# Retention and channel mix on one core: attention in 64x64 array tiles, two tokens per partition, one written order

## The chip, the cores and the metric

The kernel runs on one core of one Trainium2 chip. The metric is the device time of a launch in microseconds (us); lower is better. Engines are named as the profile does: PE is TensorE (PEld its weight loads), DVE is VectorE, ACT is ScalarE, POOL is GpSimd, SP is SyncE.

## The reference

Four sequences of 768 tokens, eight heads of 64 values. The first half is a decaying linear attention, the second a gated channel mix on its output.

```python
# attention: B, H, S, D = 4, 8, 768, 64
gamma = 1.0 - 2.0 ** (-5.0 - np.arange(H))
for t in range(S):
    state = gamma * state + outer(k[:, :, t], v[:, :, t])      # per batch and head, 64 x 64
    y[:, :, t] = (1 / sqrt(D)) * (q[:, :, t] @ state)
# channel mix: x is y with the heads side by side, 512 wide; x_prev is x one token back (0 at first)
xk = mu_k * x + (1 - mu_k) * x_prev
xr = mu_r * x + (1 - mu_r) * x_prev
k2 = relu(xk @ w_k) ** 2                                       # 512 -> 1024
out = sigmoid(xr @ w_r) * (k2 @ w_v)                           # 1024 -> 512
```

All inputs and the output are 32-bit floats in device memory.

## The kernel before

Attention works on chunks of 128 tokens, 24 of them, six to a sequence; loads and the channel mix work on blocks of 256 tokens, 12 of them. Tokens lie on the partitions: a chunk's q, k and v are tiles of 128 tokens by 8 heads by 64. q and v are loaded by GpSimd's queue and cast to 16 bits on the way, one DMA for each chunk; k comes in 32 bits through SP's queue (the first four chunks through GpSimd's).

For each chunk: `scale_k` (L179) multiplies k by powers of gamma. `transposes` (L190) turns q and the scaled k, two heads at a time, with an identity matrix on the full 128x128 array, and `transposed` (L194) copies the result from PSUM on ScalarE. `scores` (L201) multiplies k by q for each head, 64 rows of the array at a time, so that two heads use the two halves of its rows. `masked` (L209) applies the causal mask on VectorE. `state` (L222, L230) adds the chunk's k-v sums to the state in PSUM; before an even chunk the kept state is put back by a matmul with the identity. `kept` (L238) takes the state out on VectorE. `result` adds the state's part of y (L249, full array) and the chunk's own part (L255, half of the array's columns for each head). `decayed` (L266) applies the remaining decay and writes y, turned, to `xT`.

The mix has these steps for each block: `differ` (L280) takes x minus x_prev, on GpSimd except for the first two blocks; `mixed` (L288) makes xk and xr on VectorE, four instructions of 128x256 each; `keys` (L299) is xk times w_k in 32 matmuls of 256 columns; `squared` (L309, L310) is relu and square on ScalarE; `gate` (L316) is xr times w_r in 8 matmuls of 512 columns; `opened` (L323) is the sigmoid; `values` (L331) is k2 times w_v in 16 matmuls of 512 columns; `store` (L340, L345) multiplies the two on VectorE and sends the rows out by SP's queue.

PSUM's eight banks are split into two pools of four: `psa` for attention, `psm` for the mix. Each step is put in a plan with a time, from the tables `ORDER["att"]`, `ORDER["mix"]` and `ORDER["start"]` on a grid of 12 units per block; the plan is sorted by time, and every engine's instructions are written in that order. Nothing is reordered after that (`manual_schedule`).

Of the kernel before, what the change touches and what calls it, by code (L numbers as in the profile page):

```python
# [9 lines left out]
F16 = mybir.dt.float16  # L10
# [5 lines left out]
ORDER = {  # L16
    "att": {
        "scale": (-11.82,),
        "first": (-6.14, 0.23),
        "T": (-2.09, 2.5),  # L20
        "TC": (-0.47, 4.83),
        "S": (2.27, 4.47),
        "SE": (3.82, 11.21),
        "A": (3.18, 6.35),
        "M": (5.96, 7.66),
        "Y": (8.04, 9.34),
        "YE": (8.05, 9.72),
        "dx": (11.71,),
        "xk": (18.04, 21.12),
        "xr": (21.16, 27.83),  # L30
    },
    "mix": {
        "G": (-1.27, -0.4, 3.31, 4.49),
        "K": (0.71, 3.37, 5.32, 9.07),
        "R": (5.49, 5.1),
        "RS": (9.95, 9.96),
        "V": (7.7, 9.1, 4.91, 9.14),
        "O": (12.13, 13.29),
    },
    "load": (1.19, 3.99),  # L40
    "pw": (-105.55, -78.0),
    "start": {
        0: (-6.29, -4.12, -3.14, -2.71),
        1: (-5.55, -2.96, -2.96, 0.0),
        2: (-3.52, 0.96, 0.84, 1.45),
        3: (-0.17, 2.67, 1.83, 3.0),
    },
}
# [3 lines left out]
def kernel(  # L52
# [18 lines left out]
    NCH = S // C  # L71
# [3 lines left out]
    TM = 2 * C  # L75
    NBLK = B * S // TM
    COLS = S + 1
    LOG = 7
    NC = B * NCH


    gam = 1.0 - 2.0 ** (-5.0 - np.arange(H, dtype=np.float64))
    ar = np.arange(C, dtype=np.float64)
    causal_np = (ar[None, :] >= ar[:, None]).astype(np.float16)
    c16_np = np.concatenate([np.eye(P, dtype=np.float16), causal_np], axis=1)

    gk_np = np.concatenate([gam[None, :] ** (C - ar[:, None]), gam[None, :] ** (-ar[:, None])], axis=1)
    h_pj = 2 * np.arange(NJ)[None, :] + (np.arange(P) // D)[:, None]
    pw_np = gam[h_pj][:, None, :] ** (2.0 ** np.arange(LOG)[None, :, None])
    half = (np.arange(2)[None, :] == (np.arange(P) // D)[:, None]).astype(np.float64)  # L90
    one = np.ones((P, NJ))
    gs_np = np.stack([w[:, :, None] * half[:, None, :] for w in (one, gam[h_pj] ** TM)], axis=1)
    g0_np = np.stack([0.125 * KSC * gam[h_pj] ** -C, gam[h_pj] ** C], axis=1)
    small_np = np.concatenate(
        [x.reshape(P, -1) for x in (gk_np, gs_np, g0_np, pw_np)], axis=1
# [4 lines left out]
    def pool(name, bufs, **kw):  # L100
        return ctx.enter_context(tc.tile_pool(name=name, bufs=bufs, **kw))

    const = pool("const", 1)
    ld = pool("ld", 5)
    ldk = pool("ldk", 2)
    att = pool("att", 4)
    mid = pool("mid", 2)
    mix = pool("mix", 3)
    outp = pool("outp", 5)
    PS = bass.MemoryType.PSUM  # L110
    psa = pool("psa", 4, space=PS)
    psm = pool("psm", 4, space=PS)

    c16 = const.tile([P, 2 * P], F16, name="c16_sb")
    csm = const.tile([P, 2 * H + (6 + LOG) * NJ], F32, name="csm_sb")
    gy = const.tile([P, 2, NJ, C], F32, name="gy_sb")
# [7 lines left out]
    causal = c16[:, P : 2 * P]  # L124
    gk = csm[:, 0 : 2 * H].rearrange("p (e h) -> p e h", e=2)
    o = 2 * H
    gs = csm[:, o : o + 4 * NJ].rearrange("p (e j h) -> p e j h", e=2, j=NJ)
    o += 4 * NJ
    g0 = csm[:, o : o + 2 * NJ].rearrange("p (e j) -> p e j", e=2)
    o += 2 * NJ  # L130
    pw = csm[:, o:].rearrange("p (l j) -> p l j", l=LOG)
# [3 lines left out]
    K32, Q16, V16, KS, PT, QKT, PA, A2 = {}, {}, {}, {}, {}, {}, {}, {}  # L135
    PSS, SBD, PY, DX, XK, XR, K2, RS, PV = {}, {}, {}, {}, {}, {}, {}, {}, {}
    PZ, PR = {}, {}


    plan = []  # L140
    done = set()

    def needs(*marks):
        assert done.issuperset(marks), marks

    def at(t, fn, *args):
        plan.append((t, len(plan), fn, args))

    def tok(c):
        b, ci = divmod(c, NCH)  # L150
        return b, slice(ci * C, ci * C + C)


    def rows(x, n):
        b, t0 = 2 * n // NCH, 2 * n % NCH * C
        return x[b, :, t0 : t0 + TM, :].rearrange("h (c t) d -> t c h d", t=C)

    def load(n, c, x, eng, tiles, name, dt):

        if n not in tiles:  # L160
            tiles[n] = (ldk if dt is F32 else ld).tile([P, 2, H, D], dt, name=name)
        for i in range(2) if c is None else (c,):
            eng.dma_start(out=tiles[n][:, i], in_=rows(x, n)[:, i])  # L163

    def load_k(n, c=None):
        load(n, c, k, nc.sync if c is None else nc.gpsimd, K32, "k32", F32)

    def load_q(n, c=None):
        load(n, c, q, nc.gpsimd, Q16, "q16", F16)

    def load_v(n, c=None):
        load(n, c, v, nc.gpsimd, V16, "v16", F16)

    def scale_k(n, c, eng):
        if n not in KS:
            KS[n] = att.tile([P, 2, H, D], F16, name="ks16")
        e = slice(0, 2) if c is None else slice(c, c + 1)
        w = gk[:, e, :, None].to_broadcast([P, e.stop - e.start, H, D])
        eng.tensor_tensor(out=KS[n][:, e], in0=K32[n][:, e], in1=w, op=ALU.mult)  # L179
        done.update(("ks", 2 * n + i) for i in range(e.start, e.stop))  # L180

    def heads(tiles, c, a, n):
        return tiles[c // 2][:, c % 2, a : a + n, :]

    def transposes(c):
        PT[c] = psa.tile([P, 2, NJ, C], F16, name="pT", tag="a")
        needs(("ks", c))
        for i, src in enumerate((Q16, KS)):
            for j in range(NJ):
                nc.tensor.transpose(PT[c][:, i, j, :], heads(src, c, 2 * j, 2), ident)  # L190

    def transposed(c):
        QKT[c] = att.tile([P, 2, NJ, C], F16, name="qkT")
        nc.scalar.copy(out=QKT[c], in_=PT.pop(c))  # L194

    def scores(c):
        PA[c] = [psa.tile([P, NJ, C], F32, name=f"pA{hp}", tag="a") for hp in range(2)]
        for j in range(NJ):
            for hp in range(2):
                r = slice(hp * D, hp * D + D)  # L200
                nc.tensor.matmul(  # L201
                    PA[c][hp][:, j, :], lhsT=QKT[c][r, 1, j, :], rhs=QKT[c][r, 0, j, :],
                    start=(j == 0), stop=(j == NJ - 1), skip_group_check=True,
                )

    def masked(c):
        A2[c] = att.tile([P, 2, NJ, C], F16, name="a2t")
        for hp in range(2):
            nc.vector.tensor_tensor(  # L209
                out=A2[c][:, hp], in0=PA[c][hp], in1=causal[:, None, :].to_broadcast([P, NJ, C]),  # L210
                op=ALU.mult,
            )
        PA.pop(c)

    def state(c):
        needs(("ks", c))
        first = c % NCH == 0
        even = c % 2 == 0
        if even:
            PSS[c] = psa.tile([P, NJ, 2 * D], F32, name="pS", tag="a")  # L220
            if not first:
                nc.tensor.matmul(  # L222
                    PSS[c], lhsT=ident, rhs=SBD[c - 1], start=True, stop=False,
                    skip_group_check=True,
                )
        else:
            needs(("kept", c - 1))
            PSS[c] = PSS[c - 1]
        for j in range(NJ):
            nc.tensor.matmul(  # L230
                PSS[c][:, j, :], lhsT=heads(KS, c, 2 * j, 2), rhs=heads(V16, c, 2 * j, 2),
                start=(first and j == 0), stop=(j == NJ - 1), skip_group_check=True,
            )

    def kept(c):
        done.add(("kept", c))
        SBD[c] = att.tile([P, NJ, 2 * D], F16, name="sbd")
        nc.vector.tensor_tensor(  # L238
            out=SBD[c].rearrange("p j (h d) -> p j h d", h=2),
            in0=PSS[c].rearrange("p j (h d) -> p j h d", h=2),  # L240
            in1=gs[:, c % 2, :, :, None].to_broadcast([P, NJ, 2, D]), op=ALU.mult,
        )

    def result(c):
        first = c % NCH == 0
        PY[c] = psa.tile([P, NJ, C], F32, name="pY", tag="a")
        if not first:
            for j in range(NJ):
                nc.tensor.matmul(  # L249
                    PY[c][:, j, :], lhsT=SBD[c - 1][:, j, :], rhs=QKT[c][:, 0, j, :],  # L250
                    start=(j == 0), stop=False, skip_group_check=True,
                )
        for j in range(NJ):
            for hp in range(2):
                nc.tensor.matmul(  # L255
                    PY[c][hp * D : hp * D + D, j, :], lhsT=heads(V16, c, 2 * j + hp, 1),
# [25 lines left out]
    def mixed(m, dst, mu, name, half):  # L282
        xprev = shifted(m)[1]
        if m not in dst:
            dst[m] = mix.tile([P, NJ, TM], F16, name=name)
# [212 lines left out]
```

## Time and profile before

| | before |
|---|---|
| median of 3 runs | 175.91 us (175.77 to 176.37) |
| the profiled execution: span from first to last instruction | 173.1 us |
| between this span and the runs' median | 2.8 us |
| PE busy, matmuls | 155.5 us (90%), 1416 |
| DVE busy | 132.6 us (77%) |
| ACT busy | 92.3 us (53%) |
| POOL busy, its DMA issues among it | 87.7 us (51%) |
| mean granted clock of TensorE | 0.975 |

The page lists each engine's busy time and then the span in 40 slices of about 4.3 us, one digit for each: tenths of the slice in which the engine was busy, or, for PEclk, tenths of the full clock. The chain of waits goes back from the last instruction to what released each step; a row is the start, the duration and the group of instructions. In a timeline row the duration runs from the first start to the last end of the group, so rows of pipelined instructions overlap. In the groups, the last columns are busy time, mean duration of one instruction, and the idle time before them with what ended it.

### The profile page before, as it was taken

Reading aid. Unit: us, or ns where it says so; the run is one execution under the profiler, and the core shown is the slowest. Engines: PE = TensorE matmul, PEld = TensorE weight load, DVE = VectorE, ACT = ScalarE, POOL = GpSimd, SP = SyncE. Lnnn points to the kernel's source line nnn. Section 1 sums busy time; section 2 is a strip of 40 time slices with the busy share of each in tenths; the row PEclk is TensorE's granted clock in tenths of the full one; section 3 lists DMA queues with packets and bytes.
Section 4 is the critical chain, followed back from the end, with each engine's and each line's share of the span. In section 5 each row is a group of like instructions: output and inputs, shape, how many; then the busy total and the mean of one; then the engine's idle time right before and its main releaser. Section 6 shows DMA issues by size and latency. Waiting matters only on the chain.

```text
span 173.1 us, 3480 instructions
## 1 busy us (share of the span) xinstructions
PE 155.5 (90%) x1416; PEld 100.7 (58%) x1416; DVE 132.6 (77%) x232; ACT 92.3 (53%) x146; POOL 87.7 (51%) x81
## 2 busy tenths in 40 slices
PE   0367699879899999999999999999999999999990
PEld 0245457655547557758558468477476486584840
DVE  4459999858698967698799799798799696894312
ACT  3121208929223936827719719639459268275750
POOL 7999340059909990796909709629443040040000
PEclk9999957999999999999999999999999999999998
DMA  6999999997999999379892992993913011030303
GB/s 49 189 178 215 205 167 164 193 199 75 121 215 187 168 209 205 92 101 189 112 201 71 132 170 66 152 153 125 110 21 115 0 56 69 0 121 4 121 0 123
DMA packets 78496, 21.83 MB, mean 126 GB/s; under 512 B 72464, under 2 KB 75152, under 8 KB 78480
## 3 DMA queue, kind: packets, MB, share of 16 engines
q0 software_dynamic: 52880, 9.97, 67.9%
q1 hardware_dynamic: 24544, 11.64, 27.4%
q8 instruction: 11, 0.18, 0.4%
q10 hardware_dynamic: 1056, 0.00, 0.3%
q14 instruction: 5, 0.04, 0.1%
HBM read 24.22 MB, written 6.29 MB: 176 GB/s over the span
## 4 chain that ended last, share of the span: by engine, by line
PE 70%; POOL 10%; issue 8%; DMA 8%; ACT 1%; DVE 0%; POOLq 0%; DVEq 0%
PE pV L331 23%; PE pZ L299 21%; PE pR L316 10%; DMA wk<-in_moe_w_k_dram 5%; PE pT L190 5%; PE pY L255 4%; PE pA L201 3%; POOL q L163 3%; DMA v<-in_v_dram 3%; POOL ks L179 2%; PE pY L249 2%; POOL k L163 2%; POOL v L163 2%; PE pS L230 2%; POOL dx L280 1%
## 5 line engine op out<-in xcount | busy, mean ns | idle before, releaser
L280 POOL TENSOR_TENSOR dx<-xT 128x1024 f32<-128x1024 f32 x10 | 18.9, 1890 | 62.8 <-DVE xT L266 62.8
L299 PE MATMUL pZ<-xk,wk 128*128 128x256 f16 x384 | 48.6, 280 | 0.2 <-DVE xk L288 0.2
L331 PE MATMUL pV<-wv,k 128*128 128x512 f16 x192 | 46.7, 380 | 0.0
L194 ACT COPY qkT<-pT 128x1024 f16<-128x1024 f16 x24 | 24.1, 1006 | 40.8 <-PE pT L190 40.7
L299 PEld LDWEIGHTS <-wk 128*128 128x128 f16 x384 | 37.2, 100 | 7.7 <-issue 0.9
L309 ACT ACTIVATE kr<-pZ 128x512 f32<-128x512 f32 x48 | 28.4, 591 | 22.3 <-PE pZ L299 22.3
L209 DVE TENSOR_TENSOR a2t<-pA,c_sb 128x512 f16<-128x512 f32 x48 | 30.6, 681 | 10.8 <-PE pA L201 10.7
L310 ACT ACTIVATE k<-kr 128x512 f16<-128x512 f32 x48 | 30.2, 630 | 1.5
L288 DVE SCALAR_TENSOR_TENSOR xr<-dx,mur,xT 128x256 f16<-128x256 f32 x48 | 29.0, 646 | 0.0
L331 PEld LDWEIGHTS <-k 128*128 128x128 f16 x192 | 17.3, 98 | 17.9
L288 DVE SCALAR_TENSOR_TENSOR xk<-dx,muk,xT 128x256 f16<-128x256 f32 x48 | 25.4, 574 | 2.0 <-POOL dx L280 2.0
L340 DVE SCALAR_TENSOR_TENSOR osb<-pV,rsb 128x512 f32<-128x512 f32 x24 | 15.8, 684 | 11.8 <-ACT rsb L323 8.5
L316 PE MATMUL pR<-wr,xr 128*128 128x512 f16 x96 | 23.0, 379 | 0.7 <-DMA wr<-in_moe_w_r_dram 0.7
L163 POOL DMA_DIRECT2D q<-in_q_dram x24 | 22.1, 930 | 0.8 <-POOLq L482 0.8
L163 POOL DMA_DIRECT2D v<-in_v_dram x24 | 21.6, 919 | 0.0
L179 POOL TENSOR_TENSOR ks<-k,csm_sb 128x1024 f16<-128x1024 f32 x10 | 19.2, 1923 | 0.1
L266 DVE TENSOR_TENSOR xT<-pY,gy_sb 128x512 f32<-128x512 f32 x24 | 16.4, 688 | 2.9 <-PE pY L255 1.9
L323 ACT ACTIVATE rsb<-pR 128x512 f32<-128x512 f32 x24 | 13.0, 594 | 8.8 <-PE pR L316 8.7
L238 DVE TENSOR_TENSOR sbd<-pS,csm_sb 128x512 f16<-128x512 f32 x20 | 13.7, 684 | 3.6 <-PE pS L230 3.6
L316 PEld LDWEIGHTS <-xr 128*128 128x128 f16 x96 | 9.3, 98 | 11.1 <-issue 0.7
L190 PE MATMUL pT<-c_sb,q 128*128 128x128 f16 x96 | 10.1, 231 | 6.1 <-DMA q<-in_q_dram 6.1
L190 PE MATMUL pT<-c_sb,ks 128*128 128x128 f16 x96 | 10.0, 230 | 2.8 <-DVE ks L179 2.8
(29 smaller groups left out, 98.6 us busy)
## 6 DMA issues: line engine op xcount, KB each, us to landing
out_dram<-osb SPq DMA_DIRECT2D x24, 256.0 KB, 3.3
k<-in_k_dram SPq DMA_DIRECT2D x20, 256.0 KB, 6.3
q<-in_q_dram POOLq DMA_DIRECT2D x24, 128.0 KB, 5.5
v<-in_v_dram POOLq DMA_DIRECT2D x24, 128.0 KB, 7.0
k<-in_k_dram POOLq DMA_DIRECT2D x4, 256.0 KB, 5.1
wk<-in_moe_w_k_dram POOLq DMA_DIRECT2D x2, 512.0 KB, 10.4
wv<-in_moe_w_v_dram POOLq DMA_DIRECT2D x2, 512.0 KB, 20.6
wr<-in_moe_w_r_dram POOLq DMA_DIRECT2D x1, 512.0 KB, 19.8
```

What stands on the lines that cost most here:

```text
L163: eng.dma_start(out=tiles[n][:, i], in_=rows(x, n)[:, i])
L179: eng.tensor_tensor(out=KS[n][:, e], in0=K32[n][:, e], in1=w, op=ALU.mult)
L190: nc.tensor.transpose(PT[c][:, i, j, :], heads(src, c, 2 * j, 2), ident)
L194: nc.scalar.copy(out=QKT[c], in_=PT.pop(c))
L209: nc.vector.tensor_tensor(out=A2[c][:, hp], in0=PA[c][hp], in1=causal[:, None, :].to_broadcast([P, NJ, C]), op=ALU.mult,)
L280: eng.tensor_tensor(out=DX[m], in0=xcur, in1=xprev, op=ALU.subtract)
L288: nc.vector.scalar_tensor_tensor(out=dst[m][:, j], in0=DX[m][:, j], scalar=mu[:, j : j + 1], in1=xprev[:, j], op0=ALU.mult, op1=ALU.add,)
L299: nc.tensor.matmul(pZ[:, i, :], lhsT=wk16[:, co, fo * P : fo * P + P], rhs=XK[m][:, co, :], start=(i == 0 and co == 0), stop=(co == NCO - ...
L309: nc.scalar.activation(out=kr, in_=PZ.pop((m, g)), func=AF.Relu)
L310: nc.scalar.activation(out=K2[m][:, 2 * g : 2 * g + 2], in_=kr, func=AF.Square)
L316: nc.tensor.matmul(pR, lhsT=XR[m][:, co, tb * P : tb * P + P], rhs=wr16[:, co, :], start=(co == 0), stop=(co == NCO - 1),)
L331: nc.tensor.matmul(PV[m, tb], lhsT=K2[m][:, fo, tb * P : tb * P + P], rhs=wv16[:, fo, :], start=(fo == 0), stop=(fo == NFO - 1),)
```

## The change

Attention now works on blocks of 256 tokens, in 64x64 tiles of the array. Partition p of a block holds tokens 2p and 2p + 1, so a row of q, k or v in a load is 128 values (512 bytes in memory) in place of 64. The half of the partitions, u = p // 64, is a sub-chunk of 128 tokens with 64 partitions and two tokens (i) in each.

- `trans` (T): q (a = 0) and the scaled k (a = 1) are turned in pieces of 64x64, 32 for each call, and `transed` (E) copies them on ScalarE; for q it also brings the tokens back into order.
- `scores` (S), `masked` (M), `intra` (Y): the same products as before, in pieces of 64 rows by 64 columns of the array; four pieces in a row (u and the head's parity hp) lie on the four quarters.
- `state` (C) sums k times v for each sub-chunk in PSUM, without the carried state. `summed` (U) on VectorE adds the carried state to it, and `decayed` (G) on GpSimd multiplies the sum by gamma to the 128th; `inter` (I) multiplies the result with q.
- `yout` (D) writes y for the whole block in one VectorE instruction.
- All eight PSUM banks are one tile; the order names the bank of each step after an "@".
- The order of all steps is one written list; a word is a step's code and its arguments, and every engine gets its instructions in the order of the words. The tables of times, the plan and its sorting are gone.
- `differ`, `mixed`, `keys`, `squared`, `gate`, `opened`, `values` and the store compute what they did; the store's multiplication is now `result` (O), its DMA `store` (st). Block 1 takes its difference on GpSimd; only block 0 on VectorE.

```diff
-ORDER = {
-    "att": {
-        "scale": (-11.82,),
...
+ORDER = """
+lk.0 lq.0 lv.0 gy lk.2.2 lq.1 lk.1.2 ks.0.0 lv.1 lq.2 T.0.0@01 T.0.1 lv.2 E.0.0 wk.0 E.0.1 C.0@23
+wk.1 U.0.0 S.0.0@01 U.0.1 I.0.0@24 S.0.1@56 M.0.0 G.0.1 lk.4.2 M.0.1 ks.2.1 T.1.0@01 Y.0 E.1.0 D.0
+lv.4 lk.6 wr ks.1.0 dx.0.0 wv.1 T.1.1 C.1@24 E.1.1 U.1.0 X.0.0.2.3 S.1.0@01 wv.0 X.0.0.3.4
+T.2.0@25 T.2.1 X.0.0.0.1 E.2.0 M.1.0 G.1.0 I.1.0@36 E.2.1 lk.3.2 C.2@7 U.1.1 S.1.1@01 X.0.0.1.2
+S.2.0@25 M.1.1 G.1.1 M.2.0 Y.1 D.1 K.0.1@2 lq.4 U.2.0 K.0.0@5 dx.1.1 Q.0.1 Q.0.0 G.2.0 K.0.2@5
...
+V.8.1.0@6 s.8.1 M.11.1 V.8.0.0@5 X.10.0.0.1 Y.11 X.10.0.2.3 X.10.0.3.4 V.8.0.1 X.10.1.0.1 D.11
...
+st.10.1 V.11.0.0@6 O.11.1 V.11.0.1 st.11.1 V.10.0.0@5 O.11.0 V.10.0.1 st.11.0 O.10.0 st.10.0
+"""
...
-    ld = pool("ld", 5)
-    ldk = pool("ldk", 2)
...
-    psa = pool("psa", 4, space=PS)
-    psm = pool("psm", 4, space=PS)
+    PS = psum.tile([P, 8, 512], F32, name="ps")
+    Q16 = ring("q16_", 4, [H, 2 * D], F16)
+    V16 = ring("v16_", 4, [H, 2 * D], F16)
+    K32 = ring("k32_", 4, [H, 2 * D], F32)
+    KS = ring("ks_", 3, [H, 2 * D], F16)
+    QT = ring("qT_", 3, [2, NJ, C], F16)
+    KT = ring("kT_", 3, [2, NJ, 2, D], F16)
+    A2 = ring("a2_", 3, [2, 2, NJ, C], F16)
+    T32 = ring("t32_", 4, [NJ, D], F32)
+    TG = ring("tg_", 6, [NJ, D], F16)
...
     def rows(x, n):
-        b, t0 = 2 * n // NCH, 2 * n % NCH * C
-        return x[b, :, t0 : t0 + TM, :].rearrange("h (c t) d -> t c h d", t=C)
+        b, t0 = n // NB, n % NB * TM
+        return x[b, :, t0 : t0 + TM, :].rearrange("h (p i) d -> p h (i d)", i=2)
...
+    def trans(n, a, j0=0, j1=NJ):
+        pt, src = turned(n), (Q16, KS)[a](n)
+        for j in range(j0, j1):
+            for i in range(2):
+                for u in range(2):
+                    r = slice(u * D, u * D + D)
+                    for hp in range(2):
+                        nc.tensor.transpose(
+                            pt[hp * D : hp * D + D, u, j, a, i, :],
+                            src[r, 2 * j + hp, i * D : i * D + D], ident[r, r],
+                        )
...
+    def scores(n, i):
+        pa = pairs(banks("S", n, i))
         for j in range(NJ):
             for hp in range(2):
                 r = slice(hp * D, hp * D + D)
+                for u in range(2):
+                    nc.tensor.matmul(
+                        pa[u * D : u * D + D, hp, j, :], lhsT=KT(n)[r, u, j, i, :],
+                        rhs=QT(n)[r, u, j, :], ...
+                    )
...
+    def state(n):
+        for j in range(NJ):
+            for i in range(2):
+                for u in range(2 if more(n) else 1):
+                    r = slice(u * D, u * D + D)
+                    for hp in range(2):
+                        x = slice(i * D, i * D + D)
+                        nc.tensor.matmul(..., lhsT=KS(n)[r, 2 * j + hp, x], rhs=V16(n)[r, 2 * j + hp, x], ...)
+
+    def summed(n, u):
+        ...
+        if n % NB == 0 and u == 0:
+            nc.vector.tensor_tensor(
+                out=TG(2 * n + 1), in0=src, in1=gd[:, :, None].to_broadcast([P, NJ, D]), op=ALU.mult
+            )
+        else:
+            nc.vector.tensor_tensor(out=T32(2 * n + u), in0=src, in1=TG(2 * n + u), op=ALU.add)
+
+    def decayed(n, u):
+        nc.gpsimd.tensor_tensor(
+            out=TG(2 * n + u + 1), in0=T32(2 * n + u),
+            in1=gd[:, :, None].to_broadcast([P, NJ, D]), op=ALU.mult,
+        )
+
+    def inter(n, s):
+        py = pairs(banks("I", n))
+        for j in range(NJ):
+            for hp in range(2):
+                u = (1 - hp, hp)[s]
+                r = slice(hp * D, hp * D + D)
+                if more(n - 1) or u:
+                    nc.tensor.matmul(
+                        py[r, u, j, :], lhsT=TG(2 * n + u)[r, j, :], rhs=QT(n)[r, u, j, :],
+                        start=(j == 0), stop=False, skip_group_check=True,
+                    )
+
+    def intra(n):
+        py = pairs(banks("I", n))
+        inter(n, 1)
+        for j in range(NJ):
+            for i in (1, 0):
+                for u in range(2):
+                    r = slice(u * D, u * D + D)
+                    for hp in range(2):
+                        nc.tensor.matmul(
+                            py[hp * D : hp * D + D, u, j, :],
+                            lhsT=V16(n)[r, 2 * j + hp, i * D : i * D + D],
+                            rhs=A2(n)[r, i, hp, j, :], ...
+                        )
...
-    for _, _, fn, args in sorted(plan, key=lambda p: p[:2]):
-        fn(*args)
+    constants()
+    for word in ORDER.split():
+        word, _, at = word.partition("@")
+        code, *args = word.split(".")
+        args = tuple(int(x) for x in args)
+        if at:
+            key = {"T": args[:1], "I": args[:1]}.get(code, args)
+            BANK[(code,) + key] = [int(x) for x in at]
+        CODES[code](*args)
```

The codes: lk, lq, lv load k, q, v; ks is `scale_k`; dx `differ`; X `mixed` (block, xk or xr, first and last part); K `keys`; Q `squared`; R `gate`; s `opened`; V `values`; wk, wr, wv load the weights; gy builds the decay table. A second number after ks and dx picks the engine (0 VectorE, 1 GpSimd), after lk the queue (0 SP, 2 GpSimd).

## The prediction, made before the changed kernel was run

> **What bounds the kernel now.** I read the page first, then the chain of waits in order of time, the timeline of two stretches, and the groups with shapes kept apart. The page:
>
> ```profile
> span 173.1 us, 3480 instructions
> PE 155.5 (90%) x1416; PEld 100.7 (58%) x1416; DVE 132.6 (77%) x232; ACT 92.3 (53%) x146; POOL 87.7 (51%) x81
> PE   0367699879899999999999999999999999999990
> PEclk9999957999999999999999999999999999999998
> DMA packets 78496, 21.83 MB, mean 126 GB/s; under 512 B 72464, under 2 KB 75152, under 8 KB 78480
> ```
>
> TensorE is 90% busy, and from slice 12 on (about 48 us) it never rests; before that it has gaps and two slices at a lower clock. So there are two stages: a start of some 48 us that loads and VectorE set, and a rest that TensorE's own instruction stream sets. Nothing that only eases VectorE, ScalarE or GpSimd after 48 us can shorten the kernel; what shortens TensorE's stream does. The chain of waits shows a block of that stream (start us, us, what):
>
> ```profile
> 108.07 0.86 PE pV L331 x4
> 108.94 1.73 PE pR L316 x8
> 110.66 0.33 PE pA L201 x8
> 110.99 0.97 PE pV L331 x4
> 111.96 0.22 PE pY L249 x4
> 112.19 0.34 PE pY L255 x8
> 112.53 1.83 PE pV L331 x8
> ...
> 115.48 1.75 PE pZ L299 x16
> 117.23 0.22 PE pS L230 x4
> 117.45 0.45 PE pT L190 x8
> ```
>
> Three prices come out of it. A 512-column matmul costs 0.216 us (1.73/8), a 256-column one 0.109 (1.75/16), a 128-column one on the full array 56 ns (0.45/8, 0.22/4). Second: four pV after pA cost 0.97 where four elsewhere cost 0.86, so a change of array shape costs about 0.1; I take 0.095. Third: eight pA, which use half of the array's rows each, take 0.33; less one change of shape that leaves 0.23, 28 ns apiece. Two half-array matmuls share the time of one: packing by two is free in this trace. The same holds for pY of L255 (half the columns).
>
> **TensorE's sum, before.** Channel mix: 384 x 0.109 + (192 + 96) x 0.216 = 104.2 us. Attention: pT 192 x 0.056, pS 80 x 0.056 and 8 x 0.216, pY of L249 80 x 0.056, and 384 half-array matmuls x 0.028 = 32.2. Changes of shape: each chunk goes into and out of the pA shape and the pY shape, 24 x 4 less one = 95, x 0.095 = 9.0. Together 145.4; the last matmul ends at 169.1, so 23.7 us are lost at the start and to the low clock.
>
> **TensorE's sum, after.** The mix is untouched. Attention becomes 64x64 pieces: the built order holds 2688 matmuls, 672 of them mix, so 2016 of attention against 744. In groups on different tiles: transposes (T) 192 groups and block sums (C) 96, all of 64 columns; scores (S) 96, carried state (I) 96 and values (Y) 96, of 128 columns. I's groups hold one or two matmuls, C's in the last block of a batch two, the rest four. No row shows four abreast. Lower bound: packing stays free, 28 ns (half of 56) and 56 ns a group: 288 x 0.028 + 288 x 0.056 = 24.2. Upper bound: no more than the 28 ns apiece of the pairs, 112 ns for each group of four, 56 for I's: 480 x 0.112 + 96 x 0.056 = 59.1. I take 36 and 60 ns, near the lower end, because the nearest row (pA) gives up nothing for packing: 27.6. All five parts have one shape, so in the written order the stream changes shape 57 times: 5.4 us. The identity matmul that reloads the state (8 x 0.216) is gone. Sum 104.2 + 27.6 + 5.4 = 137.2, 8.2 less than before.
>
> One rule speaks against it. The Trainium skill, "TensorE: Matmul & The Clock Gate", section "Wait — 56ns, not 53.3ns?", has matmuls start no closer than about 25 ns however few their columns. Were that to hold across tiles, 2016 x 0.025 = 50.4 us would stand for my 27.6, and the forecast would be 189. The trace's 28 ns apiece lies just above that floor, so it neither shows nor refutes it.
>
> **Weight loads.** Each 64x64 piece loads its own weights (2016 loads). By the groups by shape:
>
> ```profile
> L255 PEld LDWEIGHTS <-v 128*64 128x64 f16 x192 | 6.8, 117 | 4.2 <-issue 2.4
> L201 PEld LDWEIGHTS <-qkT 64*128 64x128 f16 x192 | 5.8, 97 | 6.9 <-issue 3.6 <-ACT qkT L194 1.9 <-ACT kr L309 0.2
> ```
>
> A load of 64 columns reads 20 ns longer than one of 128. Both hide under 128-column matmuls; under 64-column ones they may not, which is why T and C carry 8 ns over their bound and S and Y only 4. The skill's "TensorEngine Tiling (Array Packing)", section "Gotcha 2: Feature Incompatibilities", says that column tiling excludes the fast weight load; these rows agree in direction, and if T and C were held to 56 ns a group by it, the sum would be 5.8 us more.
>
> **The other engines**, per block of about 12 us. VectorE: two masks and one yout of 1024 elements at 1.14 (L209 and L266 run pairs of 512 at 0.6 each, less overhead), two summed of 256 at 0.36, eight mixed at 0.40 to 0.44, two results at 0.60: 8.5 us, some 103 in all. ScalarE: two evacuations of 1.0 (L194's 1006 ns; the interleaved reading is not in the trace, and even at double price ScalarE has room), four relu-square pairs at 1.2, two sigmoids: 8. GpSimd: q and v come in half as many issues (24 instead of 48, by the row below 0.9 each: 22 us less) and the two decayed of 256 elements cost about 0.5 each (a quarter of L280's 1.89). All stay below TensorE's 11.4 and lie beside it. The issues in the page, and in the timeline a warning, mixed (L288) beside GpSimd's tensor work:
>
> ```profile
> L163 POOL DMA_DIRECT2D q<-in_q_dram x24 | 22.1, 930 | 0.8 <-POOLq L482 0.8
> ```
>
> ```profile
> 101.74 0.88 DVE L288 SCALAR_TENSOR_TENSOR xr<-dx,mur,xT 128x256 f16<-128x256 f32 x2
> ...
> 105.44 1.90 POOL L179 TENSOR_TENSOR ks<-k,csm_sb 128x1024 f16<-128x1024 f32 x1
> ...
> 106.09 1.93 DVE L288 SCALAR_TENSOR_TENSOR xr<-dx,mur,xT 128x256 f16<-128x256 f32 x2
> ```
>
> Two mixed take 0.88 alone and 1.93 beside ks, so about 1.05 us more; masks and evacuations, which read PSUM, keep their price. GpSimd's tensor operations rise from 20 to 41. If every one hit, VectorE would have 103 + 43 = 146 us from about 6 us on, still inside the kernel's time, but single waits would reach TensorE. I allow 3 us for such waits after the start, from 0 to 12.
>
> **The start.** Waits here end at loads or VectorE, so I follow the written order with this trace's durations. q, v and k of 256 tokens are one issue each (0.9 us), so wk is issued at 8.3 instead of 11.9; packets of q and v halve in number. k0 lands near 6 (here 6.4). VectorE then runs ks0, two masks, D.0, ks1, dx0, three mixed, mask, mixed, mask, with short waits in the chain transposes, evacuation, scores, mask: about 16 us, so Y.1 ends and the first keys (K.0) start at about 22.7 (23.46 in the trace). The clock is low there now:
>
> ```profile
> 24.23 2.69 PE L299 MATMUL pZ<-xk,wk 128*128 128x256 f16 x11 [0.15 <-DVE xk L288]
> ```
>
> 0.245 us a matmul instead of 0.109. I expect the same for the first keys, about 28 at their end. K.1 is ready at 27.5 (yout 1, dx 1 on GpSimd 1.9, four mixed), Y.2 ends near 33, K.2 waits for yout 2, dx 2 and four mixed until 37.7, and T.4.0 starts at about 44.7. TensorE has then done 17.4 of mix, 7.2 of attention and 0.9 of shape changes, 25.5 of its 137.2. So 111.7 remain: last matmul at 156.4, plus 3 of waits = 159.4. Behind the last matmul stand osb and the store as now, 173.1 - 169.1 = 4.0. Span 163.4. The runs' median is 175.91 against a span of 173.1, so 2.8 lie around the span: 166.2, call it 166.
>
> **Rivals.**
> A, the slower side: the tiles do not run four abreast. If only two do, groups of 64 columns cost 56 ns and of 128 columns 112 (I 56): 16.1 + 21.5 + 5.4 = 43.0, 15.4 more, 181.6; at the upper bound 198. It decides from 20 ns more per group of four (9.7 us over 480). For it: nothing past pairs was ever run here, and 128 instructions of T in a row need some 4 ns each, while pA's 16 in 0.23 us, 14 ns each, are the densest here. Against: pairs are free. Chance 0.19.
> B: TensorE waits on VectorE and GpSimd. State passes summed, decayed, summed, and decayed stands on GpSimd's queue behind loads that wait for buffers, so a late v load holds I, Y and the keys behind it; with the collisions above, about 0.9 us a block over ten blocks: 175, between 171 and 178. Chance 0.12: 0.06 faster, 0.04 the same, 0.02 slower.
> C: packing is free, the loads with half the packets leave no gap: 24.2 of attention, no later waits, two us earlier start: 166 - 3.4 - 3 - 2 = 158, from 155 to 160. Chance 0.14.
> The forecast, 160 to 171: 0.55. That the change does not do what it says is no case: the built order shows the pieces and their places.
>
> About 0.3% is what this measurement can tell from no change. Faster 0.55 + 0.14 + 0.06 = 0.75; same 0.04; slower 0.21. The faster side's own range is 155 to 174; to hold 8 in 10 I reach into A's two-abreast case: 155 to 181.
>
> **What would show it.** Right: TensorE's attention groups in the chain at about 0.29 us for a T.n.a of 32 matmuls and 0.24 for a score of 16; the first keys near 23 us; no TensorE gap over 0.5 us after 45. Wrong by A: 32 transposes in 0.45 us or more, 16 scores in 0.45. Wrong by B: TensorE waiting for mixed, masks or evacuations after 45 us, with mixed at over 0.6 us mean.

## The result, and the profile after

The changed kernel takes 205.64 us (median of 4 runs, 204.73 to 206.04) against 175.84 for the kernel before on the same chip: a ratio of 1.169 (95% interval 1.164 to 1.174). It is 30 us slower, where 166 us was forecast. The profiled execution's span is 204.1 us. Below, each time is the median of a kernel's launches in the faster of two states; the traces of e1, e2 and e12 are of slower launches, 1.6 to 1.9% above the fastest of the same kernel.

The page of the changed kernel:

```profile
span 204.1 us, 5999 instructions
PE 154.4 (76%) x2688; PEld 99.1 (49%) x2688; DVE 125.5 (62%) x192; ACT 94.4 (46%) x146; POOL 80.3 (39%) x75
PE   0363448667889965999777797899985969889992
PEclk9999999999999999699999999999999797999998
DMA packets 40425, 22.01 MB, mean 108 GB/s; under 512 B 26832, under 2 KB 36688, under 8 KB 40400
```

The DMA packets are halved, VectorE's and GpSimd's busy times fell, and every engine's share of the span fell with them. No engine became the bound. TensorE, which before never rested after slice 12, now has slices of 5 to 8 to the end: it waits, all the way through. A stretch of the chain of waits (start us, us, what) shows that the array tiles themselves do what was hoped:

```profile
62.16 0.97 PE ps L364 x4
63.13 0.35 PE ps L227 x16
63.48 0.55 PE ps L201 x64
64.02 0.97 PE ps L364 x4
64.99 0.86 PE ps L352 x4
```

Two calls of transposes, 64 matmuls, take 0.55 us: 34 ns for each group of four tiles, 8.6 ns for a matmul. Sixteen scores take 0.35, of which about 0.1 is the change of shape (the four values behind the transposes take 0.97, those four gate matmuls without a change 0.86).

To see where the time went, I cut TensorE's time up to the start of its last matmul into three: the start of the first matmul, the gaps (a matmul that starts over 0.2 us later than the one before it would need by its columns), and the rest, which is work, shape changes, low clock and smaller waits. All in us, from the traces:

| | first matmul | gaps before 80 us | gaps after 80 us | rest | last matmul starts |
|---|---|---|---|---|---|
| before | 5.2 | 12.3 | 0 | 151.2 | 168.7 |
| after | 7.8 | 27.9 | 19.6 | 144.4 | 199.7 |
| e1 (below) | 7.8 | 21.3 | 4.9 | 146.0 | 180.0 |
| e7 (below) | 7.7 | 18.5 | 5.3 | 143.1 | 174.6 |
| e12 (below) | 8.6 | 17.2 | 3.3 | 143.4 | 172.5 |

The rest fell by 6.8 us (8.1 in e7), near the 8.2 forecast. It holds the low clock too: by the granted clock at each matmul, that is about 3 us of the rest before, 4 after, 1.4 in e7 and nothing in e12. Without it the fall is 8.0 (after), 6.5 (e7) and 4.8 (e12): the step is there, and its size is known to some 3 us. The loss is in the gaps: 47.5 us where before had 12.3.

### The profile page after: what moved, and what is told of

Its sections match the earlier page's. It is cut to its first block, busy times and chain, and to the rows that moved or that the text cites. A ratio compares the mean times of both kernels' runs of the same rounds, so it can differ in the third digit from the quotient of the medians.

```text
span 204.1 us, 5999 instructions
## 1 busy us (share of the span) xinstructions
PE 154.4 (76%) x2688; PEld 99.1 (49%) x2688; DVE 125.5 (62%) x192; ACT 94.4 (46%) x146; POOL 80.3 (39%) x75
## 4 chain that ended last, share of the span: by engine, by line
PE 49%; DVE 25%; ACT 15%; issue 3%; DMA 3%; POOL 2%; SPq 0%; ACTq 0%; DVEq 0%
PE ps L338 16%; PE ps L364 15%; DVE xk L328 8%; DVE a L235 8%; DVE xT L311 7%; PE ps L352 6%; ACT qT L210 4%; ACT kT L216 4%; PE ps L201 3%; ACT k L348 3%; ACT kr L345 3%; DMA k<-in_k_dram 3%; PE ps L297 3%; PE ps L227 3%; PE ps L284 3%
## 5 line engine op out<-in xcount | busy, mean ns | idle before, releaser
L338 PE MATMUL ps<-xk,wk 128*128 128x256 f16 x384 | 50.7, 291 | 9.6 <-DVE xk L328 5.8
L364 PE MATMUL ps<-wv,k 128*128 128x512 f16 x192 | 48.1, 389 | 3.5 <-DVE xT L311 1.9
L345 ACT ACTIVATE kr<-ps 128x512 f32<-128x512 f32 x48 | 28.2, 587 | 30.1 <-PE ps L338 25.8
L235 DVE TENSOR_TENSOR a<-ps,c_sb 128x1024 f16<-128x1024 f32 x24 | 28.8, 1219 | 13.6 <-PE ps L227 5.2
L370 DVE SCALAR_TENSOR_TENSOR os<-ps,rs 128x512 f32<-128x512 f32 x24 | 16.1, 685 | 25.7 <-PE ps L364 16.1
L352 PE MATMUL ps<-wr,xr 128*128 128x512 f16 x96 | 23.4, 379 | 4.1 <-DVE a L235 2.3
L210 ACT COPY qT<-ps 128x1024 f16<-128x1024 f16 x12 | 12.1, 1012 | 30.5 <-PE ps L201 28.0
L358 ACT ACTIVATE rs<-ps 128x512 f32<-128x512 f32 x24 | 14.0, 594 | 21.6 <-PE ps L352 14.9
L311 DVE TENSOR_TENSOR xT<-ps,gy_sb 128x1024 f32<-128x1024 f32 x12 | 14.7, 1224 | 12.0 <-PE ps L297 4.5
L216 ACT COPY kT<-ps 128x1024 f16<-128x1024 f16 x12 | 12.2, 1014 | 14.7 <-DVE xT L311 6.1
```

The source lines that it names most:

```text
L210: nc.scalar.copy(out=t.rearrange("c u j (p i) -> c u j p i", i=2), in_=pt.rearrange("c u j i p -> c u j p i"),)
L216: nc.scalar.copy(out=t.rearrange("c u j i p -> c u j (i p)"), in_=pt.rearrange("c u j i p -> c u j (i p)"),)
L235: nc.vector.tensor_tensor(out=t[:, i], in0=pairs(banks("S", n, i)), in1=causal[:, i, None, None, :].to_broadcast([P, 2, NJ, C]), op=ALU.mult,)
L311: nc.vector.tensor_tensor(out=x[:, j0:j1, c : c + TM].rearrange("p j (u t) -> p u j t", u=2), in0=pairs(banks("I", n))[:, :, j0:j1], in1=g ...
L338: nc.tensor.matmul(pz[:, i, :], lhsT=wk16[:, co, fo * P : fo * P + P], rhs=XM[0](n)[:, co, :], start=(i == 0 and co == 0), stop=(co == NCO ...
L345: nc.scalar.activation(out=kr, in_=banks("K", n, g).rearrange("p (i t) -> p i t", i=2), func=AF.Relu)
```

## The experiments

Four causes were tried. **F**: false waits. All of PSUM is one tile now, and when the program is built, an instruction that reads two banks which are not neighbours (`PS[:, b0 : b1 + 1 : b1 - b0]`) is held to touch the banks between them too. So this is a matter of the waits that are written into the program, not of the chip. In the built order 66 waits among TensorE, VectorE and ScalarE are for an instruction with which the waiting one shares no bank and no data. **C**: collisions. mixed stands still beside GpSimd's work. **I**: instruction supply. TensorE stops at fixed places of its stream. **V**, added later: VectorE's amount of work.

F can be read in the timeline of the changed kernel. The three steps are V.4.0.0 into bank 4, the mask M.5.1 of banks 2 and 7, and the gate R.3.1 into bank 5, in that order (columns: start us, us, engine, line, what, and the idle time with its releaser):

```profile
98.13 1.04 PE L364 MATMUL ps<-wv,k 128*128 128x512 f16 x4
99.27 1.22 DVE L235 TENSOR_TENSOR a<-ps,c_sb 128x1024 f16<-128x1024 f32 x1 [1.07 <-PE ps L364]
100.55 1.02 PE L352 MATMUL ps<-wr,xr 128*128 128x512 f16 x4 [1.38 <-DVE a L235]
```

The mask's own scores had ended by 98.2; it waits for values in bank 4, which lies between 2 and 7. Then the gate, whose bank nobody uses, waits for the mask, because bank 5 lies there too. TensorE loses 1.38 us to a wait that no data asks for.

### e1: one instruction for each bank

```diff
 def masked(n, i):
-    nc.vector.tensor_tensor(out=t[:, i], in0=pairs(banks("S", n, i)), ...)
+    for hp in range(2):
+        nc.vector.tensor_tensor(out=t[:, i, hp], in0=PS[:, BANK["S", n, i][hp]]..., ...)
```

and the same in `transed` and `yout`.

> The changed kernel, with each instruction that read two PSUM banks at once (evacuation of T, mask, yout) cut into one instruction per bank; order, banks and arithmetic stay. Theory F (false waits): an access to banks 2 and 7 is tracked as if it covered banks 2 to 7, so 66 waits in the built order are for an instruction that touches neither the same bank nor the same data; cut in two, none is left. F expects most of TensorE's idle time to go: from 205.6 to between 160 and 178 us, the attention groups of TensorE unchanged (32 transposes about 0.3, 16 scores about 0.35), mask waits ahead of gate and values matmuls gone. Rival D (true dependences: VectorE and ScalarE are simply too slow for this order): 60 instructions more, at 0.06 to 0.1 us on VectorE (36) and 0.2 on ScalarE (24), so 205 to 213 us.

Measured: 185.45 us (183.21 to 185.91), ratio to the kernel before 1.054 (1.044 to 1.065): 20 us gained by cutting 60 instructions in two. Rival D, 205 to 213, is refuted; F's own forecast, 160 to 178, was too low. None of the 66 waits is left. The groups of gate and values, in the changed kernel and then in e1 (last columns: busy us, mean ns, idle before with its releasers):

```profile
L364 PE MATMUL ps<-wv,k 128*128 128x512 f16 x192 | 48.1, 389 | 3.5 <-DVE xT L311 1.9 <-ACT kT L216 1.1 <-DVE a L235 0.5
L352 PE MATMUL ps<-wr,xr 128*128 128x512 f16 x96 | 23.4, 379 | 4.1 <-DVE a L235 2.3 <-DVE xT L311 1.7
```

```profile
L368 PE MATMUL ps<-wv,k 128*128 128x512 f16 x192 | 46.4, 380 | 0.3 <-ACT k L352 0.2
L356 PE MATMUL ps<-wr,xr 128*128 128x512 f16 x96 | 23.4, 380 | 0.0
```

Gate and values take no data from masks or yout. The banks of e1 are those of the changed kernel, so a wait for the last reader of the same bank would have stayed; the waits that are gone are F's. F is the largest single cause. One thing more changes with it: each half of a cut read releases its bank as it ends, so a part of the 20 us can come from finer steps. And e1 is still 10 us slower than the kernel before; its gaps before 80 us are 21.3.

### e2: the same instructions, neighbouring banks

```diff
-... C.0@23 ... S.0.0@01 ... I.0.0@24 S.0.1@56 ...
+... C.0@45 ... S.0.0@67 ... I.0.0@23 S.0.1@45 ...
```

Every pair of banks in the order is renumbered so that the two are neighbours; nothing is cut.

> The changed kernel with other bank numbers after the @: every pair of banks is a neighbouring pair, so that what a pair covers is what it uses; instructions and their order stay the same on every engine. No wait in the built order is for an instruction that shares neither bank nor data. F (false waits): 157 to 175 us, at or below e1_split, for it has no extra instructions. D (true dependences): 203 to 208, as the changed kernel. If e1_split gains and this doesn't, it is not what a pair covers but which bank is used when.

Measured: 192.0 us in the one launch of the faster state (the other three 194.94 to 195.58), so no ratio can be given. That is two thirds of e1's gain or, by all four, half, with none of the 66 waits left either. F's forecast, 157 to 175, and D's, 203 to 208, both failed. Gaps fell to 35.7 only. Waits for the last reader of the same bank took the place of the false ones: values of e2 still waited 2.5 us for masks, with which they share no data, and gate 2.1 for yout. So e2 supports F in direction, and neither run is a clean price of it: e2 adds waits, e1 cuts the steps finer. Between them F is worth an estimated 14 to 20 us.

### e3: every difference on VectorE

The changed kernel has `dx` on GpSimd (1.9 us), and its chain of waits at the start reads:

```profile
30.57 1.24 DVE xT L311
31.89 1.89 POOL dx L319
33.81 5.44 DVE xk L328 x4
```

Four xk take 5.44 us, where four alone take 1.7.

```diff
 (on e1)
-... dx.1.1 ... dx.2.1 ... dx.11.1 ...
+... dx.1.0 ... dx.2.0 ... dx.11.0 ...
```

> e1_split with all differences (dx) on VectorE instead of GpSimd. Theory C (collisions: mixed stands still while GpSimd runs tensor work, on the chain before the keys of the first blocks): dx costs VectorE 1.14 instead of 1.9 plus a hand-over, and 21 us of GpSimd's tensor work are gone; e1_split's mixed of 4.6 us under dx and ks shrinks to about 2.5. 178 to 184 us against e1_split's 185.7. Rival (VectorE is simply full): 11 x 1.14 = 12.5 us more on VectorE, 186 to 195.

Measured: 181.75 us (181.42 to 181.85), ratio 1.036 (1.030 to 1.041), 3.7 below e1. Summed over all mixed of more than 0.6 us, the time beyond 0.473 (one that is not held) fell from 16.8 us (17.0 in e4, which has e1's dx) to 9.6. C's forecast holds, and its rival, a full VectorE at 186 to 195, is refuted. The 3.7 are not the price of collisions alone, since dx itself takes 1.2 in place of 1.9 on the chain; e7, below, takes collisions away without that.

### e4: the stream shifted

In e1, TensorE stops for 2.9 us (in e7, at the same place, 2.8) in the middle of `inter` with nothing to wait for (chain of waits of e1):

```profile
21.54 0.32 PE ps L287 x3
21.86 2.93 issue
24.79 0.26 PE ps L287
```

The instruction at which it resumes is number 703 of TensorE's stream (weight loads and matmuls counted); another stop lies at 2239. Both leave 191 when divided by 256.

```diff
 (on e1)
+    for i in range(160):
+        nc.tensor.transpose(PS[h : h + D, 6 + i // 2 % 2]..., ident[r, r], ident[r, r])
     for word in ORDER.split():
```

160 transposes that nobody reads, 320 instructions, run ahead of the first load's arrival.

> e1_split with 160 additional 64x64 transposes of the identity (320 TensorE instructions) before the first block, into a bank that is rewritten later; nothing reads them, and TensorE is idle then. In the changed kernel, e1_split and e2_adjacent TensorE stops at the same place of its stream, instruction 703, for 1.9 to 3.2 us at an instruction that waits for no semaphore, and at 2239 for 0.9 to 1.6. Theory I (instructions arrive too late: every 256 instructions of 64 bytes a new piece must be there, and dense 64x64 work uses it up in 1 us): the stops stay at instructions 703 and 2239 of the stream, so they move 320 instructions earlier in the work, to where TensorE waits anyhow: 181 to 185 us. Rival (something in the work itself, a bank or a buffer, stops it): the stop stays at the same matmul (inter of block 1) and the time stays at 184 to 187, or the added work costs up to 2 us.

Measured: 187.47 us (186.17 to 188.78), ratio 1.069 (1.059 to 1.079), 2.0 above e1 where 181 to 185 was forecast. The long stops are now at instructions 447, 1215 and 2495 (1.9, 1.0 and 2.0 us; shorter ones at 703 and 959), again 191 more than a multiple of 256, and in front of other work: I's claim on place holds. The time did not fall: instruction 447 lies on block 0's chain, which shows the stop,

```profile
9.45 1.63 issue
```

and the first keys begin at 28.3 as in e1. In the unshifted kernels, 16,384-byte packets on the instruction queue stand in the stops: in e7, instruction 447 was reached at 18.38, the packet ran from 22.11 to 23.04, and TensorE, which had stopped at 703 at 21.4, resumed at 24.5.

```profile
q8 instruction: 21, 0.34, 0.8%
```

That is e7's row of the queue: 21 packets for 5376 instructions, one for 256. The kernel before has 11 and no visible stop; it never takes less than 10.9 us for 256. The traces of all the versions hold 26 stops of over 0.3 us at such a place, and every one ends 1.2 to 1.6 us behind the end of a 16,384-byte packet. That is I shown by time as well as by place.

### e5: the second scaling earlier

```diff
 (on e1)
-... U.0.1 I.0.0@24 ... lk.6 wr ks.1.0 dx.0.0 ...
+... U.0.1 ks.1.0 I.0.0@24 ... lk.6 wr dx.0.0 ...
```

> e1_split with the scaling of block 1's k (ks.1) moved in the order from behind yout of block 0 to ahead of its first mask, where VectorE waits for scores. Theory S (the start is a chain of single steps on VectorE and ScalarE in the written order): ks.1 leaves the chain (1.14), block 1's transposes and evacuation run beside block 0's masks, the first keys come 2 to 4 us earlier: 181 to 184 us. Rival: the start hangs on loads or on the stop at instruction 703, then no change, 185 to 187.

Measured: 186.15 us (185.93 to 186.75), ratio 1.062 (1.056 to 1.067), no gain. VectorE then stands at block 1's k, which lands at 13.8, and the first masks behind it come late: TensorE stops for 3.9 us at 11.9. The loads set this step, not its place.

### e6: the start's edits together

```diff
 (on e1)
 e3's dx, e4's transposes, e5's ks.1
-... lq.4 ... lv.3 ... lq.3 ... lk.5.2 ... ks.4.1 ... M.2.1 ...
+... lq.4 lv.3 lq.3 lk.5.2 ... M.2.1 ks.4.0 ...
```

> e1_split with all three edits (dx on VectorE, 160 transposes ahead, ks.1 early), and further the loads of block 3 (v, q) and of k of block 5 issued right after the load of q of block 4, and ks.4 on VectorE after the mask of block 2 instead of on GpSimd, so that GpSimd runs nothing beside the mixed of blocks 0 and 1. If C, I and S each hold and their gains add: 168 to 177 us, first keys before 26 us and mixed of block 1 at 0.4 us apiece. If they hide behind each other: 178 to 183.

Measured: 183.53 us (182.8 to 183.88), ratio 1.046 (1.040 to 1.051): worse than e3 alone, and just above both forecasts. e7, which leaves e4's and e5's edits out, is 3.5 faster: the two that had failed alone cost more than the new one brought.

### e7: collisions of the start taken apart

```diff
 (on e3)
-... lq.4 ... lv.3 ... lq.3 ... lk.5.2 ... ks.4.1 ... M.2.1 ...
+... lq.4 lv.3 lq.3 lk.5.2 ... M.2.1 ks.4.0 ...
```

> As e3, but the loads v.3, q.3 and k.5 are issued by GpSimd right behind q.4, ahead of block 1's mixed, and the scaling of k for block 4 is done by VectorE behind the mask M.2.1 in place of GpSimd. Theory (mixed stands still beside GpSimd's tensor work and runs of issues): the four xk that took 5.32 us from 30.8 us take under 2.2, the chain loses about 3.3 us and pays 1.2 for the scaling on VectorE; time 178 to 180.5, mixed over 0.6 us add up to at most 6 us of excess (9.6 in e3). Rival (what is saved in the start is lost again at the next wait, for q, v or k, or for VectorE's longer queue): 181.2 or more, though the four xk are short.

Measured: 180.06 us (179.09 to 180.73), ratio 1.022 (1.018 to 1.027). The four xk, in e3's chain of waits and in e7's timeline:

```profile
30.81 5.32 DVE xk L332 x4
```

```profile
30.81 1.91 DVE L331 SCALAR_TENSOR_TENSOR xk<-dx,muk,xT 128x256 f16<-128x256 f32 x4
```

3.4 us are saved there, and 1.7 arrive at the end, as forecast; the scaling on VectorE takes 1.2.

### e8: no tensor work on GpSimd

```diff
 (on e3)
-... ks.2.1 ... ks.11.1 ...
+... ks.2.0 ... ks.11.0 ...
 def decayed(n, u):
-    nc.gpsimd.tensor_tensor(
+    nc.vector.tensor_tensor(
```

> As e3, but GpSimd does no tensor operation at all: the ten scalings of k (1.93 us there, 1.23 on VectorE) and the sixteen decayed (0.76 there, about 0.4 on VectorE) go to VectorE; GpSimd only issues DMAs. It parts two readings of the mixed that took 2.1 us under three DMA issues in a row. If the issues themselves hold VectorE, that mixed (about 31 to 34 us) stays near 2.1 us and the excess of all slow mixed is 1.7 to 3.5 us. If only tensor work holds it, none takes over 0.6 us. Time: VectorE gets 12.3 + 6.4 = 18.7 us of work and is spared 6 to 9.6; if the bare amount of VectorE's work does not matter, 179 to 182; if VectorE has become the chain, 183 to 190.

Measured: 184.76 us (184.57 to 185.59), ratio 1.052 (1.048 to 1.056): 3.0 slower than e3, by the second of the two forecasts. The groups of mixed:

```profile
L331 DVE SCALAR_TENSOR_TENSOR xk<-dx,muk,xT 128x256 f16<-128x256 f32 x48 | 20.4, 477 | 0.1
L331 DVE SCALAR_TENSOR_TENSOR xr<-dx,mur,xT 128x256 f16<-128x256 f32 x48 | 20.0, 476 | 1.0 <-PE ps L355 1.0
```

Not one of 96 is held up: 477 ns against a mean of 720 for xk in the changed kernel. So in this kernel GpSimd's tensor work is needed for a hold. It does not settle the two mixed of 2.17 and 2.12 us in the changed kernel beside which only DMA issues ran (three and four in a row, straight behind a GpSimd tensor operation): in e8 no row of issues stands straight behind a tensor operation, and the one row that met mixed, five issues, met them at its end and held neither. That stays open.

### e9: block 2 behind the first keys

```diff
 (on e7)
-... T.2.0@25 T.2.1 ... E.2.0 ... E.2.1 ... C.2@7 ... S.2.0@25 ... M.2.0 Y.1 D.1 K.0.1@2 ... K.0.0@5 ...
+... Y.1 D.1 K.0.1@7 ... K.0.0@4 T.2.0@01 T.2.1 E.2.0 C.2@2 ... E.2.1 ... S.2.0@01 ... M.2.0 ...
```

> As e7, but block 2's transposes, block sums, first scores and first mask stand behind the first keys of block 0 instead of ahead of them, in banks of their own. In e7 TensorE stopped for 3.07 us at instruction 703 of its stream (21.4 us), and a 16 KB packet on the queue that carries instructions landed at 23.04 us, in the stop; instruction 447, one piece of 256 earlier, was reached at 18.38. Theory I (a piece takes some 6 us from the crossing of the last boundary while the loads fill the DMA engines, and TensorE stops where it goes through 256 instructions faster): instruction 703 now falls at the end of the first keys, about 24 us, and the stop there shrinks to 1 us or none; VectorE is freed of a 1.2 us mask ahead of yout; first group of 32 keys begins near 25 instead of 28.0; time 175 to 178. Rival (the block's chain is only put off, and block 2's keys come later by what the first came earlier): first keys near 25, but 179 or more.

Measured: 182.36 us (181.1 to 183.07), ratio 1.044 (1.038 to 1.049). No stop over 0.3 us is left at instruction 703 or at 2239, where e7 has 5.8 us together, and the first keys begin at 25.7 in place of 28.0. Yet the kernel is 2.3 us slower: the second group of 32 keys begins at 35.1 (33.7 in e7), the third at 47.9 (44.5). The rival is right. The chain's shares, of e7 and of e9:

```profile
PE 42%; DVE 30%; ACT 14%; issue 8%; DMA 3%; SPq 0%; ACTq 0%; DVEq 0%
```

```profile
DVE 38%; PE 36%; ACT 14%; issue 6%; DMA 3%; SPq 0%; ACTq 0%; DVEq 0%
```

What the stops gave back, VectorE's share took. The edit takes the stops away and puts block 2's chain back at once, so it gives no price for the stops alone.

### e10: values moved into the second stop

```diff
 (on e9)
-... T.5.1 E.5.0 ... D.4 V.1.0.0@7 ... V.1.0.1 ...
+... T.5.1 V.1.0.0@7 V.1.0.1 E.5.0 ... D.4 ...
```

> As e9, and the 8 values of block 1, first half (V.1.0, some 1.9 us in 16 instructions), stand between the transposes of block 5 and block 6 instead of behind those of block 6, where TensorE stopped for 2.76 us at instruction 2239 (66.0 us in e7). Theory I: the piece has 1.7 to 1.9 us more to arrive, so the stop shrinks to about 1 us, and the time is 1 to 2 us below e9, 173.5 to 177. Rival: the time there is set by VectorE's mixed and yout in any case: the same as e9 within 0.5 us.

Measured: 183.25 us (181.25 to 183.74), ratio 1.047 (1.041 to 1.054), no better than e9. Moving 8 matmuls (16 instructions) brought a stop of 1.75 us back at instruction 2239, where e9 has 0.3. The two kernels reach instruction 1983 at the same time (66.8 us); the packet that follows starts at 67.4 in e9 and at 69.9 in e10, and in e7, 3.1 us behind its instruction 1983 too. So the stop comes from a late packet, not from faster work. Why the packet is late in one and not in the other, no run shows.

### e11: without xr

```diff
 (on e7)
-... X.0.1.2.3 ... X.11.1.3.4 ...        (all mixed of xr)
 def gate(n, tb):
-    lhsT=XM[1](n)[...]
+    lhsT=XM[0](n)[...]
```

> As e7, but xr is left out: its 48 mixed on VectorE (22.2 us in e7) are gone and the gate multiplies xk, with the same matmuls. It shows what VectorE's work costs. Theory V (with the false waits and the collisions gone, the written order is held by VectorE, which in e7 works 19.96 of 20 us from 80 to 100 and 19.92 from 140 to 160): TensorE's gaps after 80 us (5.3 us) go to under 1.5, those before 80 shrink by 2 to 4; time 170 to 175, below the kernel before, which still mixes xr. Rival (chains of waits through several engines, TensorE's stops at pieces of its stream and the later first matmul hold it, not the amount of VectorE's work): 177 or more, gaps after 80 us over 3.

Measured: 177.75 us (176.79 to 178.11), ratio 1.014 (1.011 to 1.017). VectorE's rows of 80 to 100 and of 140 to 160 us (columns: window, length, busy us of PE, PEld, DVE, ACT, POOL, granted clock, DMA share, GB/s), of e7 and of e11:

```profile
80.00:100.00 20.00, 18.71 (x361) 11.69 (x360) 19.96 (x33) 10.59 (x20) 7.87 (x7) 1.00 0.51 68
140.00:160.00 20.00, 19.43 (x320) 12.46 (x319) 19.92 (x38) 9.56 (x18) 1.01 (x1) 1.00 0.15 54
```

```profile
80.00:100.00 20.00, 19.07 (x307) 12.05 (x306) 16.00 (x27) 12.39 (x23) 7.84 (x7) 1.00 0.55 86
140.00:160.00 20.00, 19.62 (x290) 12.67 (x288) 15.76 (x28) 12.16 (x22) 0.00 (x0) 1.00 0.16 60
```

VectorE goes from full to 80%, and TensorE gains 0.2 to 0.4 us in each. 22 us less of VectorE's work is worth 2.3 us. The rival holds: the amount of work is not what keeps e7 above the kernel before. TensorE's gaps after 80 us are still 3.8.

### e12: the late differences back to GpSimd

```diff
 (on e7)
-... dx.6.0 ... dx.11.0 ...
+... dx.6.1 ... dx.11.1 ...
```

> As e7, but the differences of blocks 6 to 11 go back to GpSimd (1.9 us there, 1.13 on VectorE): VectorE is freed of 6.8 us in the stretches in which it is full, at the price of six GpSimd operations beside which mixed may stand still, and of 0.8 us more before each block's mixed. Theory V: 177.5 to 179.5. Rival (the longer step and the held mixed give back as much): 180 to 184, with five or more mixed over 0.6 us beside dx.

Measured: 177.48 us (175.93 to 178.05), ratio 1.008 (1.003 to 1.013), at the lower edge of V's forecast; the rival, 180 to 184, is refuted, and none of the six held a mixed. Freeing VectorE of 6.8 us here is worth 2.6 us, as much as the 22 us of e11, so where the work lies seems to count for more than its amount. It is the best version found, and still some 1% above the kernel before.

## Why the prediction was wrong, point by point

**TensorE's sum: right in what it claims, its size less sure.** It was to fall by 8.2 us; the rest of the time fell by 6.8 and, in e7, by 8.1, and without the low clock by 5 to 8. A transposes call of 32 takes 0.275 (0.29 forecast), sixteen scores 0.25 beside the change of shape (0.24). Rival A, that tiles do not run four abreast, is refuted.

**The two rules.** The floor of about 25 ns in the Trainium skill, "TensorE: Matmul & The Clock Gate", section "Wait — 56ns, not 53.3ns?", does not hold across four tiles: 64 matmuls in 0.55 us start 8.6 ns apart. By it the forecast would have been 189 us, nearer to the result, for a reason that is not there. The skill's "TensorEngine Tiling (Array Packing)", section "Gotcha 2: Feature Incompatibilities", says that column tiling excludes the fast weight load. Loads of 64x64 read 113 to 119 ns here, those of 128 columns 97 to 104. But transposes took 34 ns a group, near the 28 of free packing and well under the 56 that the prediction set against it; whether the 6 ns are the weight load's, no run shows.

**The allowance for later waits: the step that failed.** "All stay below TensorE's 11.4 and lie beside it" compared amounts of work, and then 3 us (0 to 12) were allowed for single waits. Measured, the gaps after 40 us alone are 31 us (4.1 from 40 to 60, 7.3 from 60 to 80, 19.6 after). An estimated 14 to 20 us of the whole are false waits (e1, e2). The prediction costed what each step does and where it stands; that all eight PSUM banks are one tile stands in the description of the change, but it did not ask which waits that makes. The order's bank digits showed it: S.5.1@27 holds banks 2 and 7, and whatever is written into 3 to 6 around it must wait. VectorE's amount was too low as well: 103 us were counted, and it is busy for 125.5, of which 15 are mixed that were held up.

**The start: the second step that failed.** The first keys were to begin at 22.7 and begin at 30.5. The prediction counted VectorE's operations, some 16 us from 6 us on, and put the transposes, evacuations and scores in between at "short waits". The chain has them in series with VectorE: between 9.4 and 25.8 us ScalarE's evacuations of 1,024 elements hold it five times for about 1.0 us each, k lands at 7.4 and not near 6, and TensorE's stop takes 1.6. The next step, K.1 "ready at 27.5", had dx and four mixed at some 3.5 us: they took 7.4, 5.44 of them in mixed held up.

**GpSimd beside mixed: mechanism right, place and size off.** Two mixed were to take 1.05 us more beside k's scaling, and 41 tensor operations of GpSimd were counted; the changed kernel has 37 (11 dx, 10 ks, 16 decayed). Single mixed took 1.6 to 1.9 us more (2.1 to 2.4 in place of 0.47), and in the start, where VectorE is on the chain, they counted almost in full: e7 takes 3.4 us away there, adds 1.2 and gains 1.7. e3 and e7 together gain 5.4 us, the shorter dx among it.

**Rival B** was nearest in what is seen: TensorE waits after 45 us, mixed mean 0.72 for xk. Its price, 9 us over ten blocks, is under a third of the 31 us of gaps, and its mechanism, decayed late behind loads, does not appear: GpSimd has 2% of the chain, and of TensorE's gaps 26 us end with VectorE, 15 with ScalarE and none with GpSimd.

**The rest of the loss.** e12 is still 1.008 of the kernel before. The parts are read from e7, whose last matmul starts 5.9 us later than before: the rest is 8.1 us better, the first matmul 2.5 later (it waits for q of 256 tokens in place of 128), the gaps before 80 us are 6.2 and those after it 5.3 longer. e12's trace divides in the same way, 3.8 us later with -7.8, 3.4, 4.9 and 3.3. What share of those gaps the coarser blocks alone have was not measured, and the cause of this last part stays open. In e5, e9 and e10 an edit for one gap left others of about its size.

## What to carry to other kernels

Before the amounts of work are compared, ask for each instruction what it is held to touch: a strided view over one large tile can make neighbours wait that share nothing, and a written order then has no way around. A sum by engine shows what a stage could take; with a fixed order, the chain through the engines and back decides, and it is walked step by step, evacuations included. Where several stalls lie on one chain, price each by taking it away, and ask what else the edit moved: here the edit that took 5.8 us of stops away left the kernel 2.3 us slower.

## What the runs showed of the hardware

- TensorE's instructions arrive in packets of 16,384 bytes, one for 256 instructions. TensorE stops for up to 3.2 us at an instruction that waits for nothing, always 191 past a multiple of 256, until 1.2 to 1.6 us behind a packet's end; shifting the stream by 320 moved the stops to other work (e4). All 26 stops come after 256 instructions that took 1.6 to 5.8 us (18.4 to 21.4 in e7), but other stretches of 3.2 to 4.2 us passed without one: the packet's delay decides too.
- Four 64x64 tiles at work together take one transpose each in 34 ns, and their weight loads, 117 to 119 ns each by the records, do not hold them to that time.
- A mixed on VectorE of 0.47 us that starts beside a running GpSimd tensor operation ends only behind it: 2.1 to 2.2 us beside one ks, 4.6 beside two in a row (dx, then ks, in e1; 5.0 in e4). Masks, which read PSUM, keep their time beside it (0.69 us at most in e7). With no tensor work on GpSimd, no mixed of 96 is held (e8); two in the changed kernel were held beside DMA issues alone, for a cause that stays open.
- Cutting a read of two banks in two costs VectorE 0.15 us (1,219 ns against twice 682 for a mask); with 60 reads cut, the kernel was 20 us faster.
